# Reordering matrix products by tile shape in an RWKV-5 and mixture-of-experts kernel

## The chip, the cores and the metric

The kernel runs on one core of a Trainium2 chip. The metric is the device time of one execution in microseconds (us). Before the change the median of three runs is 413.07 us (412.82 to 413.58). A profile of one execution, which the hardware profiler took, covers 410.5 us from the first to the last instruction; times within the kernel are counted from the start of that span.

Five engines work side by side: TensorE (PE; its weight loads are listed apart as PEld) multiplies matrices, VectorE (DVE) and ScalarE (ACT) work on elements and empty the accumulation banks (PSUM), GpSimd (POOL) works on elements in SBUF and issues gathers and scatters, and SyncE (SP) issues most transfers.

## What is computed

Everything is float32. An RWKV-5 attention (4 batches, 8 heads, 768 tokens, head dimension 48) feeds a layer of 8 experts, of which each token takes one.

```python
def _attn_ref(r, k, v, w, u):                    # r, k, v: (4, 8, 768, 48); w, u: (8, 48)
    for t in range(S):
        kt, vt, rt = (k[:, :, t], v[:, :, t], r[:, :, t])
        cur = np.einsum('bhd,bhe->bhde', u[None] * kt, vt)
        y[:, :, t] = np.einsum('bhd,bhde->bhe', rt, state + cur)
        state = w[None, :, :, None] * state + np.einsum('bhd,bhe->bhde', kt, vt)
    return y

def _moe_ref(x, expert_emb, tau, w1, w2):        # x: (3072, 384); w1: (8, 384, 1024)
    xn = x / (np.linalg.norm(x, axis=-1, keepdims=True) + 1e-06)
    en = expert_emb / (np.linalg.norm(expert_emb, axis=-1, keepdims=True) + 1e-06)
    logits = xn @ en.T / tau
    expert_idx = np.argmax(logits, axis=1)
    ...                                          # gate_w: softmax of the logits at expert_idx
    for e in range(E):
        mask = expert_idx == e
        h = np.maximum(x[mask] @ w1[e], 0.0)
        out[mask] = gate_w[mask, None] * (h @ w2[e])
    return out
```

## The kernel before the change

The attention is done in chunks of 128 tokens: 6 chunks of 4 batches make 24 units, `unit i` being chunk `i // 4`, batch `i % 4`. Within a chunk the decay is put into R and K (`rpow`, `kpow`), so that the chunk is a masked product of R and K times V, plus R times the state that the chunks before have left. For each unit TensorE does, by the names of the tiles that it writes:

- `rt`, `kt`: the transposes of R and of the scaled K
- `st`: what this chunk adds to the state, K times V (not in the last chunk)
- `y`: R times the state (not in the first chunk), and the masked products times V
- `at`: R times K of the next unit
- `yrows`, `xp`: the transposes of the result, back to rows and on for the router

```python
def turn_k(k, i):
    Kw = k.Kpad[i % len(k.Kpad)]
    kt = k.ps.tile([128, NP, C], F32, name="kt", tag="tp")
    for p in range(NP):
        nc.tensor.transpose(kt[:, p, :], pair(Kw, p), k.ident)
    k.KT[i] = k.work.tile([128, NP, C], F32, name="KT", tag="KT")
    nc.scalar.copy(k.KT[i], kt)

def scores(k, i):
    at = [k.ps.tile([128, NP, C], F32, name="at", tag="at") for _ in range(2)]
    for p in range(NP):
        for s in range(2):
            rows = slice(s * DP, s * DP + D)
            nc.tensor.matmul(at[s][:, p, :], KT[rows, p, :], RT[rows, p, :], start=True, stop=True)

def states(k, i):
    st = k.ps.tile([128, NP, D], F32, name="st", tag="st")
    for p in range(NP):
        for s in range(2):
            h, n = 2 * p + s, (DP, D)[s]
            nc.tensor.matmul(st[s * DP : s * DP + n, p, :], Kw[:, h, 0:n], V[:, h, :], ...)

def carry(k, i):
    ...
        nc.vector.tensor_add(T[0:PP], T[0:PP], st[0:PP])
    nc.gpsimd.tensor_mul(T[0:PP], T[0:PP], k.wC[0:PP])

def sums(k, i):
    ...                                          # R times the state, chunk 1 and later
                mm(y[s][u * DP : u * DP + n, q, :], T[s * DP : s * DP + D, p * D : p * D + n],
                   RT[s * DP : s * DP + D, p, :], ...)
    for s in range(2):
        ...                                      # masked products times V
                mm(y[s][u * DP : u * DP + n, q, :], V[:, h * D : h * D + n], AT[s][:, p, :], ...)
        nc.scalar.copy(yT[0:PP, s], y[s][0:PP])
```

The router puts each token into a list of its expert. Per chunk, `lanes` builds one-hot masks of the places in the list (VectorE), `listed` multiplies them by token numbers and gates (GpSimd, tile `what`), `taken` multiplies the two on TensorE (tile `take`, the chunk's slice of the lists), and `summed` adds it to `k.sums`. The eight PSUM banks are held by tags:

```python
    HELD = {"tp": (0, 1), "at": (2, 3), "y": (4, 5), "st": (6,), "xp": (7,), "ps": (0, 1, 6, 7, 2, 3, 4, 5)}
```

The order of one pass of the loop, cut to what is touched (`on(f, i)` calls f for unit i if there is one, `whole(f, i)` only for the last batch of a chunk, for the whole chunk):

```python
    for i in range(-1, units):
        ...
        whole(summed, i - 6)
        ...
        on(turn_r, i + 1)
        on(turn_k, i + 1)
        whole(turn_logits, i - 3)
        on(scaled, i + 2)                        # GpSimd: Kpad = K * kpow
        on(own, i + 2)                           # GpSimd: KU = K * u * R
        on(states, i)
        ...
        if j == 10:                              # unit 22
            k.lists = turned_lists(k, perm, "st")
            lists = taken_by_rank(k, k.lists)
            first = [Early(k, r, *lists, w) for r, w in zip(LAST, k.weights)]
            load_w2(k, number, k.weights[0][1])
        ...
        whole(lanes, i - 5)
        whole(listed, i - 5)
        on(own_sum, i + 1)                       # VectorE: diag = sum of KU; ScalarE scales V by it (xd)
        ...
        on(sums, i)
        whole(exps, i - 4)
        on(carry, i)
        on(scores, i + 1)
        on(masked, i + 1, 0)                     # VectorE: AT = at * mask
        on(rows, i)                              # yrows, and VectorE adds xd: X
        on(masked, i + 1, 1)
        of_group(put, i)
        of_group(turn_rows, i - 1)
        whole(logits, i - 2)
        whole(ranks, i - 3)
        whole(taken, i - 5)
```

Ahead of the loop the powers of the decay are made and the first K is turned:

```python
    nc.vector.tensor_mul(kp, t[:, :, ::-1], over_i)
    for p in range(NP):
        nc.tensor.transpose(ps[:, p].rearrange("q s d -> q (s d)"), kp[:, p, :], k.ident)
    ...                                          # rpow on ScalarE
    cols = ps[:, :, :, 0:D]
    nc.vector.tensor_mul(k.Kpad[0]..., k.loaded[0][0]..., cols)
    turn_r(k, 0)
    busy(192)                                    # [...]
    nc.vector.tensor_copy(k.kpow..., cols)
    turn_k(k, 0)
    busy(384)
```

"Early rows" are the first 128 tokens of the two experts with the longest lists. They come from the first four chunks, are gathered in unit 22, and go through their experts while the router finishes the last chunks: `Early.turn` transposes them (`early_x`), and `fill(n)` does n steps of `early_h` (times w1) or `early_y` (times w2) between the router's operations. After that all experts follow, block by block.

Of the kernel before, what the change touches and what calls it, by code (L numbers as in the profile page):

```python
# [10 lines left out]
F32 = mybir.dt.float32  # L11
# [9 lines left out]
C = 128  # L21
NCH = S // C
# [25 lines left out]
def build_first(k):  # L48


    nc, pool = k.nc, k.aconst
    wc = pool.tile([128, NP], F32, name="wc")
    nc.vector.memset(wc, 1.0)
    with nc.allow_non_contiguous_dma(reason="384 words"):
        for s, q in ((0, nc.sync), (1, nc.scalar)):
            q.dma_start(out=wc[s * DP : s * DP + D, :], in_=k.w.rearrange("(p s) d -> s d p", s=2)[s])
    k.ones = k.const.tile([128, 128], F32, name="ones")
    nc.vector.memset(k.ones, 1.0)
    wide = k.work.tile([128, 512], F32, name="wide", tag="AT1")
    nc.vector.memset(wide, 1.0)  # L60
    k.ident = k.const.tile([128, 128], F32, name="ident")
    make_identity(nc, k.ident)

    def busy(columns):
        ps = k.ps.tile([128, 512], F32, name="wake", tag="y")
        nc.tensor.matmul(ps[:, 0:columns], k.ones, wide[:, 0:columns], start=True, stop=True)

    for _ in range(WAKE):
        busy(512)
    for lst, name, count in ((k.Kpad, "Kpad", 4), (k.Rpad, "Rpad", AHEAD + 2)):  # L70
        for i in range(count):
            t = pool.tile([128, H, DP], F32, name=f"{name}{i}")
            nc.gpsimd.memset(t[:, :, D:DP], 0.0)
            lst.append(t)
    load(k, 0, nc.scalar)
    k.u_bc = pool.tile([128, H, D], F32, name="u_bc")
    nc.scalar.dma_start(
        out=k.u_bc.rearrange("p h d -> p (h d)"),
        in_=bass.AP(tensor=k.u.tensor, offset=k.u.offset, ap=[[0, 128], [1, DM]]),
    )  # L80
    for i in range(1, AHEAD - 1):
        load(k, i)
    load_rows(k)
# [12 lines left out]
    over_i = mid[:, :, None].to_broadcast([128, NP, C])  # L96
    kp = k.work.tile([128, NP, C], F32, name="kp", tag="AT0")
    nc.vector.tensor_mul(kp, t[:, :, ::-1], over_i)
    ps = k.ps.tile([128, NP, 2, DP], F32, name="kpT", tag="xp")
    for p in range(NP):  # L100
        nc.tensor.transpose(ps[:, p].rearrange("q s d -> q (s d)"), kp[:, p, :], k.ident)
    k.rpow = pool.tile([128, NP, C], F32, name="rpow")
    for p in range(NP):
        nc.scalar.mul(k.rpow[:, p, :], t[:, p, :], mid[:, p : p + 1])
    cols = ps[:, :, :, 0:D]
    nc.vector.tensor_mul(
        k.Kpad[0].rearrange("q (p s) d -> q p s d", s=2)[:, :, :, 0:D],
        k.loaded[0][0].rearrange("q (p s) d -> q p s d", s=2), cols,
    )
    turn_r(k, 0)  # L110
    busy(192)
    k.kpow = pool.tile([128, H, D], F32, name="kpow")
    nc.vector.tensor_copy(k.kpow.rearrange("q (p s) d -> q p s d", s=2), cols)
    turn_k(k, 0)
    busy(384)
    k.wC = t[:, :, C - 1 : C].to_broadcast([128, NP, D])


def numbers(k, name, shape, pattern, base, step):
    i = k.const.tile(shape, I32, name=f"{name}_i")  # L120
    k.nc.gpsimd.iota(i, pattern=pattern, base=base, channel_multiplier=step)
    f = k.const.tile(shape, F32, name=name)
    k.nc.scalar.copy(f, i)
    return f


def load_rows(k):
# [148 lines left out]
    load_w2(k, e, tiles[1])  # L276


def load(k, i, other=None):
# [7 lines left out]
    K = k.io.tile([128, H, D], F32, name="K", tag="K")  # L287
# [53 lines left out]
    nc.vector.tensor_mul(k.RT[i], rt, k.rpow)  # L341


def turn_k(k, i):

    nc = k.nc
    Kw = k.Kpad[i % len(k.Kpad)]
    kt = k.ps.tile([128, NP, C], F32, name="kt", tag="tp")
    for p in range(NP):
        nc.tensor.transpose(kt[:, p, :], pair(Kw, p), k.ident)  # L350
    k.KT[i] = k.work.tile([128, NP, C], F32, name="KT", tag="KT")
    nc.scalar.copy(k.KT[i], kt)

# [467 lines left out]
def attention(k):  # L821


    units = B * NCH

    def on(f, i, *more):
        if 0 <= i < units:
# [3 lines left out]
        if 0 <= i < units:  # L831
            f(k, k.groups[i // B], i % B)

    def whole(f, i):
        if 0 <= i < units and i % B == B - 1:
            f(k, k.groups[i // B])

    emb = build_experts(k)
    for i in range(-1, units):
        j = i - SETTLED * B  # L840
        if 0 < i + AHEAD < units:
            load(k, i + AHEAD)
        whole(summed, i - 6)
        whole(places, i - 4)
        whole(logits_out, i - 3)
        if i >= 0:
            on(turn_r, i + 1)
        if i < units - 1:
# [48 lines left out]
        whole(taken, i - 5)  # L897
        if i == 0:
            build_constants(k)
        if i == B:  # L900
            decays(k)
        if i == B + 1:
            build_turned(k)
        if 3 <= i < 3 + len(k.ring):
            k.nc.gpsimd.memset(k.ring[i - 3], 0.0)
        if j == 8:
            by = order(k, load_)
        if j == 9:
            settle(k, by, count)
            perm = turner(k, by)  # L910
        if j == 10:
            to = outs(k, lists[0], E * TM)
# [19 lines left out]
    logits_out(k, h)  # L932
    fill(1)
# [29 lines left out]
class Early:  # L963
# [12 lines left out]
        )  # L976
        self.hT = k.aconst.tile([128, NF, 128], F32, name=f"earlyh{r}")

    def turn(self):
        k, nc = self.k, self.k.nc  # L980
        ps = k.ps.tile([128, NK, 128], F32, name="early_x", tag="tp")
        for m in range(NK):
            nc.tensor.transpose(ps[:, m, :], self.G[:, m * 128 : (m + 1) * 128], k.ident)
        self.xT = k.work.tile([128, NK, 128], F32, name="earlyx", tag="KU")
        nc.vector.tensor_copy(self.xT, ps)

    def steps(self, to):

# [392 lines left out]
def all_lists(k):  # L1381

    nc = k.nc
    with ExitStack() as ctx:
        attention_pools(k, ctx)
        slots = numbers(k, "allslots", [128, SLOTS], [[1, SLOTS]], 0, 0)
        sums = k.ps.tile([128, 2, SLOTS], F32, name="allsums", tag="y")
        for c in range(NCH):
            lane, sel = slices(k, slots, *spots(k, c))
# [96 lines left out]
def kernel(  # L1486
# [34 lines left out]
    n.Rpad, n.Kpad, n.state, n.scattered = [], [], [], []  # L1521
# [43 lines left out]
```

## Time and profile before

| | us |
|---|---|
| time, median of 3 runs | 413.07 |
| profiled span | 410.5 |
| start to the first `at` | 8.70 |
| end of the early rows' products, first transposes of the experts | 165.83 |
| last scatters begin | 398.6 |

The first page of the profile gives each engine's busy time and the chain of work that ended last. The timeline lists instructions in order of time, merged where an engine does the same thing several times running; the number after `x` is how many instructions are merged. A float32 product of this kernel appears as two instructions. What stands in brackets is idle time of the engine ahead of the group, and who ended it. After TensorE's tile names stands the part of the array that is used, rows\*columns. The attention's units take about 5 us each. From some 166 us to the end, TensorE works through the experts.

### The profile page before, as it was taken

Reading aid. Unit: us, or ns where it says so; the run is one execution under the profiler, and the core shown is the slowest. Engines: PE = TensorE matmul, PEld = TensorE weight load, DVE = VectorE, ACT = ScalarE, POOL = GpSimd, SP = SyncE. Lnnn points to the kernel's source line nnn. Section 1 sums busy time; section 2 is a strip of 40 time slices with the busy share of each in tenths; the row PEclk is TensorE's granted clock in tenths of the full one; section 3 lists DMA queues with packets and bytes.
Section 4 is the critical chain, followed back from the end, with each engine's and each line's share of the span. In section 5 each row is a group of like instructions: output and inputs, shape, how many; then the busy total and the mean of one; then the engine's idle time right before and its main releaser. Section 6 shows DMA issues by size and latency. Waiting matters only on the chain.

```text
span 410.5 us, 9292 instructions
## 1 busy us (share of the span) xinstructions
PE 394.3 (96%) x3546; PEld 351.9 (86%) x3546; DVE 251.8 (61%) x605; ACT 173.0 (42%) x521; POOL 161.3 (39%) x215
## 2 busy tenths in 40 slices
PE   8999999999999899999999999999999999999980
PEld 4788788888887687899999999999999999799680
DVE  5777978767688861566767666267367266566310
ACT  4786677767777311433233332233233323232020
POOL 7997586867664323500601502310330340300220
PEclk9999999999999999999999999999999999999995
DMA  9999666667713963244705622424344250330101
GB/s 161 174 227 209 137 140 138 147 126 154 158 40 140 336 258 90 80 158 156 234 14 187 215 100 93 153 83 156 114 158 154 78 192 2 93 119 1 57 28 37
DMA packets 93800, 54.39 MB, mean 132 GB/s; under 512 B 76937, under 2 KB 88380, under 8 KB 93746
## 3 DMA queue, kind: packets, MB, share of 16 engines
q1 hardware_dynamic: 89058, 43.87, 40.1%
q0 software_dynamic: 3296, 9.44, 7.1%
q8 instruction: 30, 0.49, 0.5%
q10 hardware_dynamic: 1392, 0.39, 0.5%
q14 instruction: 24, 0.20, 0.2%
HBM read 44.45 MB, written 9.63 MB: 132 GB/s over the span
## 4 chain that ended last, share of the span: by engine, by line
PE 84%; POOL 4%; DVE 3%; issue 3%; DMA 2%; ACT 1%; POOLq 0%; SPq 0%; ACTq 0%
PE ps L1184 25%; PE ps L1248 16%; PE ps L1288 5%; PE at L362 5%; PE y L426 4%; PE ps L1302 4%; PE early_y L1003 3%; PE ps L1162 3%; PE early_h L994 3%; PE kt L350 2%; PE ps L1132 2%; PE rt L339 2%; PE st L383 2%; PE y L417 2%; PE yrows L444 2%
## 5 line engine op out<-in xcount | busy, mean ns | idle before, releaser
L1048 POOL DMA_INDIRECT out_dram<-y,to x25 | 30.2, 1206 | 173.0 <-issue 116.7
L1184 PE MATMUL ps<-xTe,w 128*128 128x192 f32 (+3 forms) x336 | 62.9, 327 | 0.0
L1184 PEld LDWEIGHTS ps<-xTe,w 128*128 128x128 f32 x336 | 55.9, 190 | 0.5
L325 ACT ACTIVATE xd<-V,diag 128x48 f32<-128x48 f32 x184 | 46.2, 326 | 1.0 <-DVE diag L316 1.0
L368 DVE TENSOR_TENSOR AT<-at,umask 128x512 f32<-128x512 f32 x48 | 32.8, 685 | 22.0 <-PE at L362 21.9
L1191 ACT ACTIVATE hT<-hT 128x384 f32<-128x384 f32 (+3 forms) x42 | 22.0, 523 | 32.4 <-DVE hT L1214 19.7
L1248 PE MATMUL ps<-Tw,Sh 128*128 128x192 f32 x192 | 32.5, 326 | 0.0
L1039 POOL DMA_INDIRECT G<-xs,take x25 | 27.5, 1098 | 10.5 <-issue 4.0
L1248 PEld LDWEIGHTS ps<-Tw,Sh 128*128 128x128 f32 x192 | 31.4, 190 | 0.0
L1184 PE MATMUL ps<-Tx,Sw 128*128 128x192 f32 (+3 forms) x168 | 29.7, 326 | 0.0
L1201 DVE TENSOR_TENSOR u<-ps,p 128x384 f32<-128x384 f32 (+3 forms) x14 | 7.8, 558 | 32.9 <-ACT p L1198 16.4
L362 PE MATMUL at<-RT,KT 48*128 48x128 f32 x384 | 27.9, 285 | 0.0
L1184 PEld LDWEIGHTS ps<-Tx,Sw 128*128 128x128 f32 x168 | 27.6, 190 | 0.1
L362 PEld LDWEIGHTS at<-RT,KT 48*128 48x128 f32 x384 | 23.3, 187 | 4.9 <-ACT xd L325 2.0
L426 PE MATMUL y<-AT,V 128*48 128x128 f32 (+1 forms) x384 | 26.2, 277 | 0.0
L310 POOL TENSOR_TENSOR KU<-KU,Rpad 128x384 f32<-128x384 f32 x24 | 24.1, 1006 | 1.9
L309 POOL TENSOR_TENSOR KU<-K,u_bc 128x384 f32<-128x384 f32 x24 | 24.1, 1006 | 1.5 <-DMA u_bc<-in_u_dram 1.5
L532 ACT COPY xT<-xp 128x384 f32<-128x384 f32 x24 | 11.5, 479 | 30.3 <-PE xp L530 30.3
L1248 PE MATMUL ps<-w,hT 128*128 128x192 f32 x128 | 23.4, 326 | 0.0
L426 PEld LDWEIGHTS y<-AT,V 128*48 128x48 f32 (+1 forms) x384 | 20.1, 124 | 3.5 <-issue 3.4
L301 POOL TENSOR_TENSOR Kpad<-K,kpow 128x384 f32<-128x384 f32 x23 | 23.0, 1002 | 0.0
L1211 ACT ACTIVATE hT<-ps 128x384 f32<-128x384 f32 (+3 forms) x14 | 6.9, 491 | 35.7 <-PE ps L1184 35.7
(239 smaller groups left out, 816.3 us busy)
## 6 DMA issues: line engine op xcount, KB each, us to landing
w<-in_moe_w_dram SPq DMA_DIRECT2D x16, 1536.0 KB, 6.9
K<-in_k_dram SPq DMA_DIRECT2D x24, 192.0 KB, 3.7
V<-in_v_dram SPq DMA_DIRECT2D x24, 192.0 KB, 4.3
xs<-X SPq DMA_DIRECT2D x24, 192.0 KB, 2.3
Rpad<-in_r_dram SPq DMA_DIRECT2D x23, 192.0 KB, 4.2
G<-xs,take POOLq DMA_INDIRECT x27, 3.2
out_dram<-y,to POOLq DMA_INDIRECT x25, 3.7
Rpad<-in_r_dram ACTq DMA_DIRECT2D x1, 192.0 KB, 4.3
```

The lines of the kernel that those rows point to most:

```text
L301: k.nc.gpsimd.tensor_mul(k.Kpad[i % len(k.Kpad)][:, :, 0:D], k.loaded[i][0], k.kpow)
L309: nc.gpsimd.tensor_mul(KU, K, k.u_bc)
L310: nc.gpsimd.tensor_mul(KU, KU, R[:, :, 0:D])
L325: k.nc.scalar.mul(k.xd[i][:, h, :], V[:, h, :], diag[:, h : h + 1])
L362: nc.tensor.matmul(at[s][:, p, :], KT[rows, p, :], RT[rows, p, :], start=True, stop=True)
L368: k.nc.vector.tensor_mul(a, k.at[i][s], k.umask[:, None, :].to_broadcast([128, NP, C]))
L426: mm(y[s][u * DP : u * DP + n, q, :], V[:, h * D : h * D + n], AT[s][:, p, :], start=(c == 0 and q == 0), stop=True, skip_group_check=True,)
L1039: nc.gpsimd.indirect_dma_start(out=G[0:n, :], out_offset=None, in_=k.xs[:, :], in_offset=IndirectOffsetOnAxis(ap=take[0:n], axis=0), bound ...
L1048: put = k.nc.gpsimd.indirect_dma_start(out=k.out[:, :], out_offset=IndirectOffsetOnAxis(ap=to, axis=0), in_=y, in_offset=None, bounds_chec ...
L1184: nc.tensor.matmul(ps[:, j, :], weights[:, (f + j) * 128 : (f + j + 1) * 128], moving, start=(first and j == 0), stop=True, skip_group_che ...
L1191: nc.scalar.activation(h, h, ACT.Relu)
L1248: nc.tensor.matmul(ps, a[:, f, :], b[:, f, :], start=(first and f == 0), stop=(f == NF // 2 - 1), skip_group_check=True)
```

## The change

The change moves `states` from ahead of the products with the state to behind the products with V, and moves `taken` behind `states`, one unit later than before and into another bank. These three groups use all rows of the array and half of its columns. `summed` moves behind `carry`.

Ahead of the loop the first K is loaded straight into its padded tile and transposed as it came; the decay is multiplied in when VectorE empties the bank, in place of ScalarE's copy. K itself is scaled in place afterwards. The casts of the router's number tables wait until after `rpow` on ScalarE, and one waking matmul goes away.

In unit 22 the load of the first early expert's w2 moves from ahead of the gathers' next work to behind `put`. After the loop, the early rows are transposed ahead of the last rows of the router; the first copy goes to ScalarE, the masks of the chunk before last are built ahead of the second copy, and one `fill(1)` is added ahead of `logits`.

```diff
-    load(k, 0, nc.scalar)
+    load(k, 0, nc.scalar, k.Kpad[0])
 ...
-    nc.vector.tensor_mul(kp, t[:, :, ::-1], over_i)
+    nc.vector.tensor_mul(kp, t[:, :, ::-1], mid[:, :, None].to_broadcast([128, NP, C]))
+    k.rpow = pool.tile([128, NP, C], F32, name="rpow")
+    for p in range(NP):
+        nc.scalar.mul(k.rpow[:, p, :], t[:, p, :], mid[:, p : p + 1])
+    cast(k)
+
+    kt = turned_k(k, 0)
+    k.KT[0] = k.work.tile([128, NP, C], F32, name="KT", tag="KT")
+    nc.vector.tensor_mul(k.KT[0], kt, kp)
+    turn_r(k, 0)
     ps = k.ps.tile([128, NP, 2, DP], F32, name="kpT", tag="xp")
     for p in range(NP):
         nc.tensor.transpose(ps[:, p].rearrange("q s d -> q (s d)"), kp[:, p, :], k.ident)
 ...                                            (rpow's old place)
-    nc.vector.tensor_mul(
-        k.Kpad[0].rearrange("q (p s) d -> q p s d", s=2)[:, :, :, 0:D],
-        k.loaded[0][0].rearrange("q (p s) d -> q p s d", s=2), cols,
-    )
-    turn_r(k, 0)
     busy(192)
     k.kpow = pool.tile([128, H, D], F32, name="kpow")
-    nc.vector.tensor_copy(k.kpow.rearrange("q (p s) d -> q p s d", s=2), cols)
-    turn_k(k, 0)
-    busy(384)
+    nc.vector.tensor_copy(k.kpow.rearrange("q (p s) d -> q p s d", s=2), ps[:, :, :, 0:D])
+    first = k.Kpad[0].rearrange("q (p s) d -> q p s d", s=2)[:, :, :, 0:D]
+    nc.vector.tensor_mul(first, first, ps[:, :, :, 0:D])
 ...                                            (the loop)
-        whole(summed, i - 6)
 ...
-        on(states, i)
 ...
-            load_w2(k, number, k.weights[0][1])
 ...
         on(sums, i)
+        on(states, i)
+        whole(taken, i - 6, "xp")
         whole(exps, i - 4)
         on(carry, i)
+        whole(summed, i - 6)
         on(scores, i + 1)
 ...
         of_group(put, i)
+        if j == 10:
+            load_w2(k, number, k.weights[0][1])
         of_group(turn_rows, i - 1)
         whole(logits, i - 2)
         whole(ranks, i - 3)
-        whole(taken, i - 5)
 ...                                            (behind the loop)
     load_weights(k, expert_number(k, LAST[1]), k.weights[1])
+    first[0].turn(nc.scalar.copy)
     gates(k, g)
-    first[0].turn()
+    lanes(k, g)
+    listed(k, g)
+    first[1].turn(nc.vector.tensor_copy)
     turn_rows(k, h, B - 1)
     squares(k, h, B - 1)
-    first[1].turn()
-    lanes(k, g)
-    listed(k, g)
     norms(k, h)
+    fill(1)
     logits(k, h)
     logits_out(k, h)
     fill(1)
```

More of the change, by code (lines that the diff above doesn't have):

```diff
@@ L95, in build_first @@
     nc.vector.reciprocal(mid, t[:, :, C // 2])
-    over_i = mid[:, :, None].to_broadcast([128, NP, C])
     kp = k.work.tile([128, NP, C], F32, name="kp", tag="AT0")
-    nc.vector.tensor_mul(kp, t[:, :, ::-1], over_i)
+    nc.vector.tensor_mul(kp, t[:, :, ::-1], mid[:, :, None].to_broadcast([128, NP, C]))
[7 more added lines that the diff above has]
+    turn_r(k, 0)
     ps = k.ps.tile([128, NP, 2, DP], F32, name="kpT", tag="xp")
@@ L101, in build_first @@
         nc.tensor.transpose(ps[:, p].rearrange("q s d -> q (s d)"), kp[:, p, :], k.ident)
[L102 to L105, printed above, removed]
-    nc.vector.tensor_mul(
-        k.Kpad[0].rearrange("q (p s) d -> q p s d", s=2)[:, :, :, 0:D],
-        k.loaded[0][0].rearrange("q (p s) d -> q p s d", s=2), cols,
-    )
-    turn_r(k, 0)
     busy(192)
     k.kpow = pool.tile([128, H, D], F32, name="kpow")
-    nc.vector.tensor_copy(k.kpow.rearrange("q (p s) d -> q p s d", s=2), cols)
-    turn_k(k, 0)
-    busy(384)
+    nc.vector.tensor_copy(k.kpow.rearrange("q (p s) d -> q p s d", s=2), ps[:, :, :, 0:D])
+    first = k.Kpad[0].rearrange("q (p s) d -> q p s d", s=2)[:, :, :, 0:D]
+    nc.vector.tensor_mul(first, first, ps[:, :, :, 0:D])
     k.wC = t[:, :, C - 1 : C].to_broadcast([128, NP, D])
@@ L122, in numbers, with cast @@
     f = k.const.tile(shape, F32, name=name)
-    k.nc.scalar.copy(f, i)
+    k.casts.append((f, i))
     return f
+def cast(k):
+    for f, i in k.casts:
+        k.nc.scalar.copy(f, i)
+    k.casts.clear()
 def load_rows(k):
@@ L276, in load_weights, with load @@
     load_w2(k, e, tiles[1])
-def load(k, i, other=None):
+def load(k, i, other=None, K=None):
     nc = k.nc
@@ L285, in of @@
         return src[b, :, c * C : (c + 1) * C, :].rearrange("h s d -> s h d")
-    K = k.io.tile([128, H, D], F32, name="K", tag="K")
+    K = k.io.tile([128, H, D], F32, name="K", tag="K") if K is None else K[:, :, 0:D]
     nc.sync.dma_start(out=K, in_=of(k.k))
@@ L341, in turn_r, with turned_k @@
     nc.vector.tensor_mul(k.RT[i], rt, k.rpow)
-def turn_k(k, i):
-    nc = k.nc
+def turned_k(k, i):
     Kw = k.Kpad[i % len(k.Kpad)]
@@ L349, in turn_k @@
     for p in range(NP):
-        nc.tensor.transpose(kt[:, p, :], pair(Kw, p), k.ident)
+        k.nc.tensor.transpose(kt[:, p, :], pair(Kw, p), k.ident)
+    return kt
+def turn_k(k, i):
+    nc = k.nc
+    kt = turned_k(k, i)
     k.KT[i] = k.work.tile([128, NP, C], F32, name="KT", tag="KT")
@@ L821, in attention @@
 def attention(k):
-    units = B * NCH
+    nc, units = k.nc, B * NCH
     def on(f, i, *more):
@@ L832, in of_group, with whole @@
             f(k, k.groups[i // B], i % B)
-    def whole(f, i):
+    def whole(f, i, *more):
         if 0 <= i < units and i % B == B - 1:
-            f(k, k.groups[i // B])
+            f(k, k.groups[i // B], *more)
     emb = build_experts(k)
@@ L977, in __init__, with turn @@
         self.hT = k.aconst.tile([128, NF, 128], F32, name=f"earlyh{r}")
-    def turn(self):
+    def turn(self, copy):
         k, nc = self.k, self.k.nc
@@ L984, in turn @@
         self.xT = k.work.tile([128, NK, 128], F32, name="earlyx", tag="KU")
-        nc.vector.tensor_copy(self.xT, ps)
+        copy(self.xT, ps)
     def steps(self, to):
@@ L1386, in all_lists @@
         slots = numbers(k, "allslots", [128, SLOTS], [[1, SLOTS]], 0, 0)
+        cast(k)
         sums = k.ps.tile([128, 2, SLOTS], F32, name="allsums", tag="y")
@@ L1519 @@
     n.need_dram = tc.dram_tile([E, TG], I32, name="need_dram")
-    n.Rpad, n.Kpad, n.state, n.scattered = [], [], [], []
+    n.Rpad, n.Kpad, n.state, n.scattered, n.casts = [], [], [], [], []
     for name in ("loaded", "KU", "diag", "xd", "RT", "KT", "at", "AT", "st", "y", "groups"):
```

## The prediction

> **What bounds the kernel now.** I read the first page for the busy shares, then the waits of TensorE, then its timeline unit by unit, because the change mostly reorders TensorE's work. The page says that one engine is nearly always busy and that the chain that ended last runs mostly through it:
>
> ```profile
> PE 394.3 (96%) x3546; PEld 351.9 (86%) x3546; DVE 251.8 (61%) x605; ACT 173.0 (42%) x521; POOL 161.3 (39%) x215
> PE 84%; POOL 4%; DVE 3%; issue 3%; DMA 2%; ACT 1%; POOLq 0%; SPq 0%; ACTq 0%
> ```
>
> TensorE's own list of waits adds up to only 3.4 us (the longest is 1.6 us before the first matmul). So there is little waiting to remove; the time is TensorE's sequence itself and how closely its products follow each other. The next view is TensorE's timeline over one unit of the attention (one chunk of 128 tokens of one batch) and the start of the next. Columns: start, busy time, engine, line, tile written and read, rows\*columns of the array, number of instructions.
>
> ```profile
> 51.18 0.49 PE L530 MATMUL xp<-ident,X 128*128 128x128 f32 x3
> 51.51 0.60 PE L339 MATMUL rt<-ident,Rpad 128*128 128x128 f32 x4
> 52.15 0.63 PE L350 MATMUL kt<-ident,Kpad 128*128 128x128 f32 x4
> 52.71 0.67 PE L383 MATMUL st<-V,Kpad 128*64 128x48 f32 x16
> 53.30 0.65 PE L417 MATMUL y<-RT,state 48*64 48x128 f32 x16
> 53.89 1.08 PE L426 MATMUL y<-AT,V 128*48 128x128 f32 x16
> 54.90 1.16 PE L362 MATMUL at<-RT,KT 48*128 48x128 f32 x16
> ...
> 56.43 0.49 PE L530 MATMUL xp<-ident,X 128*128 128x128 f32 x3
> 56.85 0.66 PE L692 MATMUL take<-lane,what 128*64 128x128 f32 x8
> 57.44 0.66 PE L339 MATMUL rt<-ident,Rpad 128*128 128x128 f32 x4
> 57.94 0.60 PE L350 MATMUL kt<-ident,Kpad 128*128 128x128 f32 x4
> 58.47 0.67 PE L383 MATMUL st<-V,Kpad 128*64 128x48 f32 x16
> ```
>
> The shape after the tile names is what matters: st is 128\*64, the product with the state is 48\*64, the product with V is 128\*48 (both V and st occupy all rows and half of the columns), at is 48\*128. I then took, from the same trace, the distance from the start of a group's last matmul to the start of the next group's first. Where the shape stays, it is 0.11 us (rt to kt at its least, kt to lg) and under 0.06 us between st and V. Where it changes it is 0.20 us after a matmul with 128 moving columns (kt to st, V to at, at to yrows, xp to take, take to rt), and 0.15 us after one with 48 (st to the product with the state). So a change of shape costs about 0.09 to 0.10 us more than a close follower. In the first chunk, where no product with the state stands between, st and V already lie together:
>
> ```profile
> 20.37 0.61 PE L383 MATMUL st<-V,Kpad 128*64 128x48 f32 x15
> ...
> 21.85 0.83 PE L362 MATMUL at<-RT,KT 48*128 48x128 f32 x10
> ```
>
> That is 1.48 us for st and V together, from the first start to the start of at. It is the number that I use for the new order.
>
> [...] groups seem to overlap by 0.07 us (st at 52.71 plus 0.67 ends after 53.30); so I reckon from start to start. [...] That bears on the early rows' gathers, which land after 6.1 to 6.4 us while an expert's weights move, against a median of 3.2 us for all gathers.
>
> **The change part by part.**
>
> *States next to the products with V.* Nothing is removed; the same instructions stand in another order. Old order from kt: kt, st, state product, V, at. New: kt, state product, V, st, at. Old time from the start of st: 53.30 − 52.71 = 0.59 to the state product, then 53.89 − 53.30 = 0.59 to V, then 54.90 − 53.89 = 1.01 to at; together 2.19. New: 0.59 for the state product, then 1.48 for V and st; together 2.07. The move into the state product from kt costs the same change of shape as that into st. Gain 0.12 us per unit. It applies where both st and a state product exist: chunks 1 to 4, four units each, so 16 units: 1.9 us. It is all on the path, since nothing else ends the units. Chunk 0 has no state product and gains nothing; chunk 5 has no states.
>
> Two units have another product of full shape between st and what follows. The fourth unit has the experts' transposes between st and V (st at 25.00, transposes at 25.59, V at 25.87, at at 26.89, after kt at 24.44, thus 2.45 from kt to at). New: about 0.43 from kt to these transposes (as from kt to lg), 0.28 to V, 1.48 to at: 2.19, gain 0.26. The unit with the count (cp at 115.55) saves one more change of shape, gain about 0.1 above its 0.12.
>
> *Slices (take) next to them.* Four times in the loop. Out of its present place: the pair of shape changes and the eight matmuls take 56.43 to 57.44 where a plain unit has 51.18 to 51.51, which is 1.01 against 0.33. But in the plain unit kt then stands back: 52.15 − 51.51 = 0.64 from rt to kt, against 57.94 − 57.44 = 0.50 after take. There kt waits until VectorE has read yrows, whose bank it gets. To st, the unit with take is 58.47 − 56.43 = 2.04 and the plain one 52.71 − 51.18 = 1.53, so take now really costs 0.51. In the new place it costs eight matmuls at 0.055, 0.44[...]. I count 0.05 us each, 0.2 in all.
>
> *The first K turned as it came.* Here I expected most and get least. The chain to the first at now: kp, its transposes, the product into Kpad (0.56), transposes of K, the copy on ScalarE (0.59), at:
>
> ```profile
> 8.06 0.59 ACT L352 COPY KT<-kt 128x512 f32<-128x512 f32 x1 [1.19 <-PE kt L350]
> 9.67 1.91 ACT L325 ACTIVATE xd<-V,diag 128x48 f32<-128x48 f32 x8 [1.03 <-DVE diag L316]
> 11.49 0.56 ACT L352 COPY KT<-kt 128x512 f32<-128x512 f32 x1
> ```
>
> New: K is transposed as soon as the waking matmuls end (6.09), one VectorE product makes KT (start 6.75, 0.6 to the next start), then RT, so at can start near 8.1 instead of 8.70. That is 0.6 us. But the second at (12.29) waits for the second of these KT copies, which stands on ScalarE behind eight products xd, which wait for diag, which waits for GpSimd's KU at 9.05. None of these four is made earlier, and VectorE has to do kpow and the scaling of K before diag, ending about 9.05 too. So 0.1 us is left at the second at. Moving the casts behind rpow (eight, 1.4 us on ScalarE) serves the same chain and adds nothing.
>
> *Early rows.* Two waits are listed here: the first early_x for its gather, take for `what`:
>
> ```profile
> 138.94 0.55 PE L983 MATMUL early_x<-ident,G 128*128 128x128 f32 x3 [0.40 <-DMA G<-xs,take]
> 139.56 0.55 PE L530 MATMUL xp<-ident,X 128*128 128x128 f32 x3
> ...
> 143.09 0.66 PE L692 MATMUL take<-lane,what 128*64 128x128 f32 x8 [0.52 <-POOL what L673]
> 143.68 1.60 PE L994 MATMUL early_h<-earlyx,w 128*128 128x128 f32 x12
> ```
>
> The w2 load moves behind the unit's other work, from 130.18 to about 136, so both gathers (issued at 132.5 and 134.2) should land before they are asked for. But xp at 139.56 waits for VectorE's X, which ends at 139.35, and the second early_x has to wait for that too, since it gets the bank of yrows. So the end of that wait brings almost nothing. What does bring something is one step of early_h (three products) put between xp and lgT, while ScalarE copies xT; 12 matmuls are two steps and take 1.44 us, so a step is 0.72. And take no longer waits 0.52, since lane and sel come before the second copy; of that about 0.4 goes to the step now ahead of it. I count 0.8 us for both. The total of early_h and early_y is unchanged, and TensorE stays busy from there to the experts, so this reaches the end.
>
> Sum: 1.9 + 0.36 + 0.2 + 0.1 + 0.8 = 3.4 us, from 413.07 to 409.7. The experts' part, from 166 us on, has the same instructions and no waits of TensorE in the list.
>
> **The rivals.** First: the cost of a shape change is not the change but the close of a dependency, and it reappears elsewhere. st now comes last ahead of at, and carry reads it on VectorE. For this rival: VectorE has to finish carry (0.35) before it masks at. Against: at takes 1.1 us, VectorE idles 1.7 us there waiting for it, so carry and the addition of the slices (0.26) fit. It would leave the attention at zero: about 412. Second: GpSimd becomes the bound, since the state's decay (0.51) starts 0.8 us later in each unit and K's scaling stands behind it. Its work is about 3.5 us of a unit's 5.2, and scaled K is used one unit later, so I give it little; it would cost up to 2 us in the crowded first units: 411 to 413. Third: the later w2 is late for early_y at 149, or slows the load of the next expert's weights (issued at 140.5). 1.5 MB at 370 to 400 GB/s (the windows from 132 to 140 us) take 4 us, so it lands about 141; time 409.7 unchanged unless the queue stands still. Fourth, on the good side: all of the 0.6 us at the start comes through (0.5 more than counted), and take's two shape changes (0.2 for each of the four, 0.6 more than counted): 408.6.
>
> **Range and chances.** The surest term is the 1.9 us, known to 0.03 us per unit, thus 0.5 in all. The others may be from 0 to about twice their size. That gives 408.3 to 411.3. To be faster by over 2% the time would have to fall under 404.8, over twice the sum; slower by 2% is above 421.3, which needs a new wait in every unit.
>
> **What would show it.** Right: in chunks 1 to 4, from the state product to at 2.07 us with no st ahead; the second at near 12.2; TensorE's wait for `what` gone; the experts' first transposes about 3.4 us earlier than 165.99, near 162.6. Wrong: a wait of TensorE for carry, KT or Kpad in every unit, V to at over 1.5 us, or a gap ahead of early_y.

## The result, and the profile after

Before: 413.34 us (median of five runs, 412.82 to 413.99). After: 408.76 us (five runs, 408.67 to 409.36). The ratio is 0.9892, with a 95% interval from 0.9877 to 0.9906: 1.08% less time, some 4.5 us (3.9 to 5.1). 409.7 had been predicted, with 408.3 to 411.3 as the range.

The two profiled executions stand closer together than the medians: spans of 410.5 and 407.2 us, 3.3 us apart. That of before took 413.07 us, 0.27 less than its median, and that of after was its longest run (409.36, 0.60 over its median). In a second set of runs (after_again, below) the change was worth 3.5 us by the medians. So the timelines are used here for what each part did, and the medians for what it was worth.

The page of after, its busy line and the engines' shares of the chain that ended last:

```profile
PE 390.2 (96%) x3544; PEld 352.6 (87%) x3544; DVE 254.0 (62%) x605; ACT 170.8 (42%) x521; POOL 161.9 (40%) x215
PE 88%; DVE 3%; issue 2%; ACT 1%; DMA 1%; POOL 1%; ACTq 0%; POOLq 0%
```

TensorE's busy time fell by 4.1 us (394.3 to 390.2), with two instructions less (one waking product, 0.81 us): the rest went out of the time of the same matmuls. By their listed lengths the groups overlap (in the view below, V from 53.13 with 1.08 us runs to 54.21, and st starts at 54.04), so I again reckon from start to start. TensorE's timeline in after: a plain unit, and from the next one the part with the slices.

```profile
51.99 0.63 PE L353 MATMUL kt<-ident,Kpad 128*128 128x128 f32 x4
52.54 0.66 PE L427 MATMUL y<-RT,state 48*64 48x128 f32 x16
53.13 1.08 PE L436 MATMUL y<-AT,V 128*48 128x128 f32 x16
54.04 0.61 PE L393 MATMUL st<-V,Kpad 128*64 128x48 f32 x16
54.58 1.16 PE L372 MATMUL at<-RT,KT 48*128 48x128 f32 x16
...
59.14 0.56 PE L393 MATMUL st<-V,Kpad 128*64 128x48 f32 x15
59.51 0.30 PE L702 MATMUL take<-lane,what 128*64 128x128 f32 x1
59.53 0.22 PE L393 MATMUL st<-V,Kpad 128*64 128x48 f32 x1
59.59 0.62 PE L702 MATMUL take<-lane,what 128*64 128x128 f32 x7
60.14 1.16 PE L372 MATMUL at<-RT,KT 48*128 48x128 f32 x16
```

From the state product to at are 2.04 us (54.58 − 52.54); 2.07 had been predicted, and the old order took 2.19 from st to at. The group st now follows V without a step (it starts 0.91 after V, whose listed length is 1.08). The slices even run mixed with the last st; both have the shape 128\*64.

The start of after. The first at comes at 8.08 (before: 8.70), but the second at 12.38 (before: 12.29). In between, the transposes of the second K (kt) wait for Kpad on GpSimd:

```profile
6.10 0.60 PE L353 MATMUL kt<-ident,Kpad 128*128 128x128 f32 x4
8.08 1.16 PE L372 MATMUL at<-RT,KT 48*128 48x128 f32 x16 [0.18 <-DVE RT L346]
10.33 0.66 PE L353 MATMUL kt<-ident,Kpad 128*128 128x128 f32 x4 [0.45 <-POOL Kpad L306]
12.38 1.16 PE L372 MATMUL at<-RT,KT 48*128 48x128 f32 x16
```

The early rows in after. A step of early_h (x6) stands between the second xp and lgT, and take waits for nothing:

```profile
134.94 0.85 PE L454 MATMUL yrows<-ident,yT 112*128 112x112 f32 x4
...
135.95 0.49 PE L995 MATMUL early_x<-ident,G 128*128 128x128 f32 x3
136.98 0.55 PE L995 MATMUL early_x<-ident,G 128*128 128x128 f32 x3 [0.54 <-DVE X L460]
137.37 0.49 PE L540 MATMUL xp<-ident,X 128*128 128x128 f32 x3
137.69 0.83 PE L1006 MATMUL early_h<-earlyx,w 128*128 128x128 f32 x6
...
140.22 0.66 PE L702 MATMUL take<-lane,what 128*64 128x128 f32 x8
```

The wait for a gather is gone; what TensorE waits for here now is X, 0.54 us by the second early_x. Where the 3.5 us between the two traces arose can be read from the start of each unit's at, before minus after (a unit's at stands in the pass of the unit before it): −0.09 at the second at, which is unit 1's, +0.14 at unit 6, 0.02 at unit 7, 1.49 at unit 16, 2.35 at unit 20, 2.42 at unit 23; 3.53 at the experts' first transposes (165.83 to 162.29) and 3.53 at the last matmul. In between, the states gave 0.15 us in 13 of the 16 passes with a state product, 0.34 in the one with the count, and 0.13 ahead of these 16 in the pass with the experts' transposes; the four slices 0.25 in all, and the early rows 1.11. The passes of units 5 and 6 lost 0.12 each, as two waits came up that were not there before:

```profile
37.26 1.16 PE L372 MATMUL at<-RT,KT 48*128 48x128 f32 x16 [0.20 <-ACT xd L330]
43.44 1.16 PE L372 MATMUL at<-RT,KT 48*128 48x128 f32 x16 [0.20 <-DVE mx L579]
```

The engines named do not seem to end the wait: at reads RT, and VectorE makes RT from 36.44 to 37.11 and from 42.61 to 43.29 here, behind small table operations, once-only work that is put into these two passes. "further" below tests this.

### The profile page after: what moved, and what is told of

Read it like the earlier page. It is cut to its first block, busy times and chain, and to the rows that moved or that the text cites. A ratio compares the mean times of both kernels' runs of the same rounds, so it can differ in the third digit from the quotient of the medians.

```text
span 407.2 us, 9284 instructions
## 1 busy us (share of the span) xinstructions
PE 390.2 (96%) x3544; PEld 352.6 (87%) x3544; DVE 254.0 (62%) x605; ACT 170.8 (42%) x521; POOL 161.9 (40%) x215
## 4 chain that ended last, share of the span: by engine, by line
PE 88%; DVE 3%; issue 2%; ACT 1%; DMA 1%; POOL 1%; ACTq 0%; POOLq 0%
PE ps L1196 25%; PE ps L1260 16%; PE at L372 6%; PE ps L1300 5%; PE y L436 5%; PE ps L1314 4%; PE kt L353 3%; PE early_h L1006 3%; PE early_y L1015 3%; PE yrows L454 3%; PE ps L1174 3%; PE y L427 2%; PE ps L1144 2%; PE rt L344 2%; PE st L393 2%
## 5 line engine op out<-in xcount | busy, mean ns | idle before, releaser
L314 POOL TENSOR_TENSOR KU<-K,u_bc 128x384 f32<-128x384 f32 x23 | 23.1, 1003 | 0.0
```

The lines of the kernel that those rows point to most:

```text
L314: nc.gpsimd.tensor_mul(KU, K, k.u_bc)
```

## Experiments

Unit shifts are starts of at, read as above; the first four kernels are the old one with a single part of the change.

**states_only.** States behind the products with V, all else old.

```diff
-        on(states, i)
         of_group(squares, i - 1)
 ...
         on(sums, i)
+        on(states, i)
```

> Only states moves behind the products with V; all else is as before. If the time is TensorE's sequence and one change of shape less saves 0.12 to 0.15 us in each of 16 units, and the units with the experts' transposes and with the count save 0.2 to 0.3 more together: 2.2 us less than before. If the gaps are really waits that move elsewhere (carry, GpSimd's scaling of K): within 0.5 us of before.

Measured: 411.66 us beside 413.12, ratio 0.9966 (0.9953 to 0.9978), 1.4 us less. Its trace is ahead of before by 2.1 us at the last unit with states, and loses 0.27 again at the gathers, which now come too late by more: 1.1 us of waiting by the first early_x (0.4 in before), and the experts begin 1.81 earlier. So the units' own gain is about as large as in after, and part of it runs into the old order of the early rows.

**taken_only.** Slices behind the products with V, and their addition behind carry.

```diff
-        whole(summed, i - 6)
 ...
         on(sums, i)
+        whole(taken, i - 6, "xp")
         whole(exps, i - 4)
         on(carry, i)
+        whole(summed, i - 6)
 ...
-        whole(taken, i - 5)
```

> Only take moves next to the products with V (states stays ahead of the product with the state), and its addition behind carry. Sequence theory: 0.2 us less than before, no more, as kt then stands back for VectorE's read of yrows in the units that lose take. If each of its two changes of shape counted in full: 0.8 us less.

Measured: 412.67 (412.55 without two of the 16 runs, which took 575.86 and 1389.25 and are left out of the ratio), ratio 0.9991 (0.9981 to 1.0002). In the trace each of the four slices gives 0.07 to 0.08 us, 0.28 from the second at to the last; in the time that can't be told from nothing.

**first_only.** The first K loaded straight into its padded tile and turned as it came, with the scaled K made after it, and the casts later; of the edit, only the turning and the scaling are shown.

```diff
+    kt = turned_k(k, 0)
+    k.KT[0] = k.work.tile([128, NP, C], F32, name="KT", tag="KT")
+    nc.vector.tensor_mul(k.KT[0], kt, kp)
     turn_r(k, 0)
 ...
-    turn_k(k, 0)
-    busy(384)
+    first = k.Kpad[0].rearrange("q (p s) d -> q p s d", s=2)[:, :, :, 0:D]
+    nc.vector.tensor_mul(first, first, ps[:, :, :, 0:D])
```

> Only the first K's part and the delayed casts. Sequence theory with the second at as the bound: the first at 0.6 us earlier, the second at within 0.1 us of before, total within 0.2 us of before. If the start were a chain of its own: 0.6 us less.

Measured: 413.11, ratio 0.9996 (0.9988 to 1.0004). Its trace has the second at at 12.37 and then loses 0.36 us at the gathers (two waits of early_x, 1.2 us in all). Alone this part gives nothing that can be measured.

**early_only.** The w2 load later, and the early rows' copies, lanes and step of early_h in the new order.

```diff
-            load_w2(k, number, k.weights[0][1])
 ...
         of_group(put, i)
+        if j == 10:
+            load_w2(k, number, k.weights[0][1])
 ...
+    first[0].turn(nc.scalar.copy)
     gates(k, g)
-    first[0].turn()
+    lanes(k, g)
+    listed(k, g)
+    first[1].turn(nc.vector.tensor_copy)
     turn_rows(k, h, B - 1)
     squares(k, h, B - 1)
-    first[1].turn()
-    lanes(k, g)
-    listed(k, g)
     norms(k, h)
+    fill(1)
```

> Only the early rows' part: w2's load behind put, the two transposes together, the copies and masks reordered, one step of early_h ahead of the logits. Sequence theory: 0.8 to 1.1 us less than before, all of it between 137 and 146 us. If part of the whole change's gain comes from transfers and shows nowhere in the sequence of TensorE: 1.5 to 2.2 us less, with a difference after 166 us.

Measured: 412.1, ratio 0.9972 (0.9964 to 0.998), 1.2 us less; in the trace this stretch is 1.11 us shorter, as in after. The pieces of the new order (the first copy on ScalarE, the masks ahead of the second copy, the added step) were not run apart.

**w2_only and w2_back.** What of the 1.11 us belongs to the later load, and what to the order? w2_only is the old kernel with the load of w2 moved alone (the first two hunks of early_only); w2_back is the changed kernel with that load at its old place.

> The kernel before with the later load of w2 alone. If the late gathers cost what the run with w2's load put back showed: early_x no longer waits for G, and the time falls by 0.5 to 1.3 us. If the rest of that stretch (the last rows, take's masks) bounds it anyway, so that the two parts only pay together: 0 to 0.4 us less.

> The changed kernel with w2's load back at its early place. If the gathers do not matter, because the rows of the last unit are waited for anyway (the prediction): within 0.2 us of the changed kernel. If the gathers then land late by varying amounts, and swallow what was gained ahead of them: 0.4 to 1.2 us more, with a wait of early_x for G.

Measured: w2_only 413.27 beside 412.97, ratio 1.0001 (0.9993 to 1.001): nothing. Its gathers are early, but xp then waits 1.0 us for ScalarE's xT (in this trace X itself comes late, see after_again). w2_back 410.67, ratio 0.995 (0.9931 to 0.9969), which is 1.7 us more than states_ahead_v (408.99, below, which runs as after does) on the same chip. TensorE's timeline of w2_back:

```profile
135.41 0.85 PE L454 MATMUL yrows<-ident,yT 112*128 112x112 f32 x4
...
137.63 0.55 PE L994 MATMUL early_x<-ident,G 128*128 128x128 f32 x3 [1.04 <-DMA G<-xs,take]
138.75 0.52 PE L994 MATMUL early_x<-ident,G 128*128 128x128 f32 x3 [0.58 <-DVE sel L669]
139.11 0.49 PE L540 MATMUL xp<-ident,X 128*128 128x128 f32 x3
```

From yrows to the second xp are 3.70 us (139.11 − 135.41), in after 2.43 (137.37 − 134.94): 1.27 us are lost here (another 0.47 of this trace is its later start). The second wait is put down to sel on VectorE; the view of the gathers' tile speaks for the transfer. In w2_back:

```profile
L983 POOL DMA_INDIRECT G<-xs,take x2: 998/1158/1318, 130.6 to 132.2; - x2
...
DMA to landing us min/median/max: 6.4/6.7/7.0
```

The gathers are issued at 130.6 and 132.2 and land 7.0 and 6.4 us later, thus at 137.6 and 138.6, where the two early_x begin. (Which of the two figures belongs to which gather the view does not say; taken so, both fit.) In after:

```profile
DMA to landing us min/median/max: 3.7/4.3/4.9
```

So the new order without the later load would give 1.11 − 1.27 = −0.16 us, the later load without the new order about −0.1 in its trace and nothing in the median, and both together 1.11. The two only pay together: each takes away one of two waits that lie side by side: the load alone leaves the wait for xT, the order alone the wait for the gathers.

**no_first.** The changed kernel with the first K and the casts as before (first_only's hunks undone).

> The changed kernel with the first K's part and the delayed casts undone. If that part is worth nothing, as the run with it alone said: within 0.2 us of the changed kernel (408.8). If it takes away a start that varies (the first at at 8.7 to 9.35 us, by the moment at which TensorE gets its full clock), and the run with it alone lost that again at the gathers: 0.4 to 0.6 us more, and more spread between runs.

Measured: 409.94, ratio 0.9913 (0.9896 to 0.993), by the medians 0.95 us above states_ahead_v on the same chip, with intervals that overlap. In its trace the second at comes at 13.54, in after at 12.38, and this stays to the end (1.20 at the experts' first transposes). Yet before had it at 12.29 with the same start-up code. TensorE's first group of waking matmuls (tile wake, which nothing reads) in no_first,

```profile
1.64 5.49 PE L66 MATMUL wake<-wide,ones 128*128 128x512 f32 x6 [1.64 <-DVE wide L60]
```

and the same six in before:

```profile
1.64 4.58 PE L66 MATMUL wake<-wide,ones 128*128 128x512 f32 x6 [1.64 <-DVE wide L60]
```

They start at the same moment, and in no_first take 0.9 us longer (4.62 in after). What differs is the moment at which TensorE gets its full clock. The record of the granted clock that each trace holds begins with full clock at 5.18 us in before, 5.26 in after and 7.83 in no_first, and the products' pace changes there: the four transposes kpT still ran in the slow stretch in no_first and took 0.86 us to the next group (6.92 to 7.78), in before 0.46 (6.09 to 6.55). The second at by that moment:

| start-up | full clock from, us | second at, us |
|---|---|---|
| old | 4.78, 5.18, 6.44, 6.62, 7.37, 7.83 | 12.41, 12.29, 12.86, 12.95, 13.32, 13.54 |
| new | 4.63, 5.26, 5.71, 6.28, 7.08, 7.23 | 12.37, 12.38, 12.38, 12.39, 12.79, 12.86 |

Where the full clock comes near 5.2, the new start is 0.1 us later; where it comes later, the new start is about 0.4 us earlier at like moments (12.39 at 6.28 beside 12.86 at 6.44; 12.86 at 7.23 beside 13.32 at 7.37). (Left out are further, which changes the start itself, and states_behind_at, which has other products ahead of the second at.) So of no_first's 1.16 us an estimated 0.4 is the old start, and the rest the late clock.

**after_again.** The changed kernel once more, beside states_split, w2_only and further.

> The changed kernel once more, for the same chip and runs of before: 0.989 of before, about 408.8 us; the second at at 12.4 us unless the waking matmuls end after 6.6 us.

Measured: 409.5 (409.05 to 410.21), ratio 0.9909 (0.9896 to 0.9923). Between the medians that is 3.5 us less than before (3.8 by the ratio). Its profiled execution got its full clock late, at 7.08 (the waking took 5.49 us again), and had its second at at 12.79. In the units its trace repeats that of after, but the early rows give only 0.53 us here, as X on VectorE comes late:

```profile
137.82 0.55 PE L995 MATMUL early_x<-ident,G 128*128 128x128 f32 x3 [0.87 <-DVE X L460]
```

In after this wait is 0.54. X starts 0.80 and 1.18 us after the last product of yrows in units 22 and 23, in after 0.37 and 0.85. The traces of further and w2_only, from the same chip, show the same lateness; why stays open.

**states_ahead_v and states_split.** Does it matter that st stands behind V, or only how often the shape changes? states_ahead_v puts st between the state product and V (as few changes of shape as in after); states_split puts half of st ahead of the state product and half behind V (one more change), with the same instructions.

```diff
-        on(sums, i)
-        on(states, i)
+        on(states, i, 0)
+        on(sums, i)
+        on(states, i, 1)
```

> The changed kernel with states between the product with the state and the products with V. The shapes change as often as in the changed kernel. Shape theory: within 0.3 us of the changed kernel (408.8). If st's place behind V matters (copies of y start earlier there): 0.5 us more or worse, with waits of yrows for yT.

> The changed kernel with half of states (pairs 0 and 1) back ahead of the product with the state, the other half behind V. Nothing of st is later than in the changed kernel, so carry and GpSimd are as there; the shapes change five times per unit of chunks 1 to 4 in place of four. Shape theory: 0.15 us per unit in 16 units, 2.4 us more than the changed kernel, seen unit by unit. Dependency theory: as the changed kernel within 0.5 us.

Measured: states_ahead_v 408.99, ratio 0.9902 (0.9886 to 0.9917), its trace ends within 0.08 us of that of after (0.13 to 0.14 us a unit in place of 0.15, and less lost in the two passes that wait for RT). states_split 411.37, ratio 0.9963 (0.9948 to 0.9977), 1.87 us above after_again on the same chip; its trace falls back by 0.12 to 0.13 in 13 of the 16 passes, by 0.17 in one, and not at all in the two in which at waits for RT; 1.8 in all. A unit of states_split:

```profile
52.83 0.43 PE L395 MATMUL st<-V,Kpad 128*64 128x48 f32 x8
53.19 0.65 PE L428 MATMUL y<-RT,state 48*64 48x128 f32 x16
53.78 1.08 PE L437 MATMUL y<-AT,V 128*48 128x128 f32 x16
54.69 0.38 PE L395 MATMUL st<-V,Kpad 128*64 128x48 f32 x8
```

The same 16 products st, cut in two by the other shape, bring back most of what the change had gained in the units (1.8 of 2.3 us). The number of changes of shape is the cause, not st's place.

**states_behind_at.** A control meant to have st between at and yrows, so that shapes change as often as before. For this, carry has to stand behind the second mask.

```diff
         on(sums, i)
-        on(states, i)
 ...
-        on(carry, i)
         whole(summed, i - 6)
         on(scores, i + 1)
+        on(states, i)
         on(masked, i + 1, 0)
         on(rows, i)
         on(masked, i + 1, 1)
+        on(carry, i)
```

> The changed kernel with states between at and yrows, carry behind the second mask. There st is as late as in the changed kernel but has no neighbour of its shape: five changes of shape per unit again (one more in chunk 0). Shape theory: 2.5 to 3 us more than the changed kernel, about 411.5. If it is only being later that helps (dependencies): as the changed kernel within 0.5 us. If GpSimd's decay of the state were close to being the bound: over 413.

Measured: 437.61, ratio 1.057 (1.0547 to 1.0592). Of the three cases put down, only the last allows it (over 413, if GpSimd's decay were close to being the bound), and it is far above that. Another chain forms. TensorE's waits in it:

```profile
PE kt L353 <- DVE X L460: 7.6, 5, 2.2
PE rank L609 <- DVE state L408: 5.4, 4, 1.4
PE lgT L556 <- DVE state L408: 4.0, 3, 1.3
```

and from 40 to 100 us GpSimd's wait for carry, 19.2 us (longest 5.3), where after has 7.2 (longest 3.9):

```profile
POOL state L409 <- DVE state L408: 19.2, 6, 5.3
```

These waits fit a chain in which carry comes late on VectorE, GpSimd's decay of the state and K's scaling behind it come late, and the next units' transposes wait. The granted clock fell too: it is 0.50 from 41 to 44, from 68 to 71 and from 150 to 156 us (0.96 as the mean from 40 to 130), where after has it full (1.00) throughout the units. So the run tells nothing of shapes. It does show what the second rival of the prediction looks like where it binds, with st behind at and carry behind the second mask; which of the two moves brings it about was not run apart.

**further.** If the two waits for RT in units 5 and 6 come from table work on VectorE, this work can go where VectorE is freer: behind diag in the passes of units 5, 9 and 13, with build_turned cut in two (build_more makes mask, turned and tie). The kernel also loads u ahead of the first V, on SyncE's queue, as GpSimd's KU waits for it at the start (1.5 us in before).

```diff
+        if i == B + 1:
+            no_counts(k)
+            decays(k)
+        if i == 2 * B + 1:
+            build_turned(k)
+        if i == 3 * B + 1:
+            build_more(k)
 ...
-        if i == B:
-            decays(k)
-        if i == B + 1:
-            build_turned(k)
```

> The changed kernel with u loaded ahead of the first V, so that GpSimd can begin KU sooner, and with the decays' test and the router's number tables moved on VectorE from the ends of units 4 and 5 to behind diag in units 5, 9 and 13, where it waits for st. Sequence theory: the waits of at for RT in units 5 and 6 go (0.3 us in all), the second at moves from 12.4 to about 11.7 us (0.7 us): 1 us less than the changed kernel. If at waits for ScalarE's copy at the start all the same: 0.3 us less.

Measured: 407.83 (407.48 to 408.56), ratio 0.9871 (0.9855 to 0.9886), 1.67 us less than after_again on the same chip: faster than both kernels. TensorE in further, in the second of the two units:

```profile
43.53 1.16 PE L381 MATMUL at<-RT,KT 48*128 48x128 f32 x16
44.63 0.60 PE L463 MATMUL yrows<-ident,yT 112*128 112x112 f32 x4
45.06 0.49 PE L549 MATMUL xp<-ident,X 128*128 128x128 f32 x3
45.40 0.31 PE L618 MATMUL rank<-seq,umask 128*128 128x32 f32 x2
```

The same in after_again:

```profile
43.85 1.16 PE L372 MATMUL at<-RT,KT 48*128 48x128 f32 x16 [0.20 <-DVE mx L579]
44.94 0.60 PE L454 MATMUL yrows<-ident,yT 112*128 112x112 f32 x4
45.38 0.49 PE L540 MATMUL xp<-ident,X 128*128 128x128 f32 x3
46.13 0.41 PE L609 MATMUL rank<-seq,umask 128*128 128x32 f32 x2 [0.26 <-DVE state L408]
```

At 37 us further is level with after_again (37.61 and 37.66 at the start of at), two units later 1.09 us ahead (48.80 and 49.89). As further had begun 0.22 later (second at at 13.01), the tables were worth 1.3 us, far more than the two listed waits of 0.2 each: rank after xp (0.75 against 0.34) and kt after rt (0.69 against 0.47) waited too, in part without a releaser shown. Both passes whose at had waited for RT now gain their 0.15 like the others, so this work was the cause of the two waits. The early rows give 0.67 us here, with a wait for X of 0.9, much as in after_again (0.53), where after has 1.11. The earlier u brought nothing at this trace's late clock (full from 7.53); it was not run by itself. That the whole came near the 1 us put down is luck: 0.7 had been expected from the start and 0.3 from the tables.

## Why the prediction held, and where its steps did not

*States (1.9 + 0.26 + 0.1 = 2.26 predicted; 2.42 + 0.09 − 0.25 = 2.26 in the trace, from the second at to unit 23's, without the slices).* Right in its cause, the changes of shape; that the size fits so well is luck, as errors cancel. 13 passes gave 0.15 us instead of 0.12, and the one with the count 0.34 instead of 0.22. Two passes lost 0.12 instead of gaining it, and the one with the experts' transposes gave 0.13 instead of 0.26: these transposes do not have the full shape that the prediction ascribes to them (the trace has 8\*128), and kt to them took 0.57 (24.47 to 25.04) where 0.43 had been taken. states_split shows the cause: with one change more in each of 16 units it took 1.87 us more by the medians (1.8 in the traces, 0.12 to 0.13 a unit in all but three of them). What TensorE does at such a change the runs do not show. It stayed on the path, as reckoned: V and st took 1.45 us where 1.48 was borrowed from chunk 0. The missed part was RT: the move brings at nearer to its RT, and VectorE was late with it in two passes.

*Slices (0.2).* 0.25 in the trace of after, 0.28 in that of taken_only: right, though too small for the medians alone. The 0.05 for each was an estimate, put a little under the 0.51 − 0.44 = 0.07 that the trace of before gave; taken_only shows 0.07 to 0.08.

*First K (0.1).* That GpSimd's chain leaves little of the 0.6 us at the second at came true, but the prediction named another step of it. It has the second at wait for ScalarE's copy of KT; in its own trace this copy ends at 12.05 (11.49 + 0.56), 0.24 us ahead of at, and no wait is shown there. In after it is kt that waits, 0.45 us for Kpad; the copy runs from 11.76 to 12.32, just ahead of at at 12.38. The size was read from one trace with an early full clock. The term is −0.1 there and about 0.4 where the clock comes late. Of the sum's terms this one was sized worst, because it has no single size.

*Early rows (0.8).* 1.11 in the trace of after, 0.53 in that of after_again, and the reason given failed in one step: "So the end of that wait brings almost nothing", of the gathers, as xp waits for X anyway. True of the old order (w2_only: nothing), false of the new (w2_back: 1.27 us lost). The step counted each wait against the old order of the others, where the later load and the new order only pay together.

*The rivals.* That the cost reappears in carry did not happen: no wait of TensorE for carry is new in after. GpSimd's chain did not bind in the units either (states_behind_at shows what it would have looked like). w2 was not late for early_y: 3.53 us are kept from the early rows to the last matmul. The good side came about in part: some more of the start comes through wherever the full clock comes late. The sign "near 162.6" was reckoned from 165.99; the trace has 165.83, and after 162.29.

*The total.* 3.4 predicted; 3.5 between the traces, 4.5 (3.9 to 5.1) between the medians, and 3.5 between those of after_again (3.2 to 4.3 by the ratio's interval). The profiled runs are 0.27 us under and 0.60 us over their medians, which makes up most of the difference between traces and medians. Gathers vary in such runs too: the first early_x comes 1.58 us after yrows in before's trace, 1.76 to 2.32 in the others with the early w2, and 1.01 to 1.14 in those with the late one. Why after's profiled run was its longest, with an early start, is not shown. Not settled: the four single parts add up by their ratios to 0.75% (0.34 + 0.09 + 0.04 + 0.28), the whole is 1.08%, in after_again 0.91%. The loss of states_only and first_only at the gathers (0.27 and 0.36 us in their traces) explains some of it, but the runs do not close the sum.

## What to carry to other kernels

Where TensorE is busy all the time, put products that use the array alike side by side (here 128\*48 beside 128\*64: in before under 0.06 us from the last product's start to the next one's, where a change of shape took 0.15 to 0.20) and count the changes; check each time that what reads the moved products on other engines still has its slack. Read two adjacent waits as one question, since removing one may only uncover the other. And before sizing a term from a start-up or a gather, look at several traces for how much that moment moves by itself, and at when the clock rises in each.

## What the runs showed of the hardware

**The full clock moves.** The record of the granted clock begins with full clock at 4.63 to 7.83 us in the fourteen traces, which is 2.99 to 6.19 us after the first matmul (1.64). The same six first matmuls take 4.31 to 5.49 us, as their weight loads fall from 0.34 to 0.19 us earlier or later or not at all; with the old start-up the second at, and the kernel behind it, shifts by up to 1.2 us (12.29 to 13.54). So the moment moved by 3.2 us between runs that began with the same six products; what sets it is not shown.

**A small cast on VectorE ended with a product of GpSimd.** The cast of 128x3 numbers took 0.87 us in after and 2.54 us in states_behind_at. VectorE's timeline of states_behind_at,

```profile
45.47 2.54 DVE L203 CAST own<-bits 128x3 f32<-128x3 int32 x1
```

and GpSimd's:

```profile
46.02 1.00 POOL L306 TENSOR_TENSOR Kpad<-K,kpow 128x384 f32<-128x384 f32 x1
46.98 1.01 POOL L314 TENSOR_TENSOR KU<-K,u_bc 128x384 f32<-128x384 f32 x1
48.07 1.00 POOL L315 TENSOR_TENSOR KU<-KU,Rpad 128x384 f32<-128x384 f32 x1
```

The cast ends at 48.01, at the end of GpSimd's second product (47.99). In after it ran from 41.00 to 41.87 beside a product of GpSimd from 40.85 to 41.85, in before from 40.97 to 41.84 beside one from 40.82 to 41.82. The ends agree in all three runs (within 0.02 us), but in states_behind_at the cast lasted across several instructions of GpSimd, not one. Why they end together is not shown. In these runs table work of a few elements so held RT up by more than its size suggests (the next operation, of 128x1, took 0.16 us in after); how much of further's gain is this was not measured.
